# Query features of sketch attention formed by token from 8-vectors: a fused attention and GELU kernel on one core

## The chip, the cores and the metric

The kernel runs on one core of one Trainium2 chip. The metric is the time of one execution on the device in microseconds (us). The engines are named as the profile names them: PE is TensorE (matrix products), PEld its loading of weights, DVE is VectorE, ACT is ScalarE, POOL is GpSimd, and SP is SyncE, whose queue issues the DMAs.

## The reference

Polynomial sketch attention feeds a GELU block. The sizes are 4 batches, 4 heads, 1088 tokens, head width 32, and sketches of 8 rows; the GELU block takes 4352 tokens of width 128 through 2048 hidden units.

```python
def phi(x):
    a = np.einsum('rd,bhsd->bhsr', S1, x)
    b = np.einsum('rd,bhsd->bhsr', S2, x)
    return np.einsum('bhsi,bhsj->bhsij', a, b).reshape(*x.shape[:-1], r * r)
q_p, k_p = (phi(q), phi(k))
kv = np.einsum('bhsf,bhsd->bhfd', k_p, v)
z = np.sum(k_p, axis=2)
num = np.einsum('bhsf,bhfd->bhsd', q_p, kv)
den = np.einsum('bhsf,bhf->bhs', q_p, z)[..., None] + 1e-06
x = (num / den) by token, heads side by side      # 4352 x 128
...
h = x @ w_in
g = 0.5 * h * (1.0 + erf(h * inv_sqrt2))
out = g @ w_out
```

The 64 features of a token are the outer product of two 8-vectors a and b, so the denominator is also the sum over i of a_i times c_i, where c is z (as an 8x8 matrix) applied to b, or in the other order a sketch of the query whose rows are mixed by z. The weights come as double words and are rounded to f32 in the kernel.

## The kernel before, in words

**Chunks.** The queries are taken in nine chunks. Chunks n = 0 to 7 hold 512 tokens of all four heads each, two chunks a batch; chunk 8 is the remainder, the last 64 tokens of each of the four batches (256 columns). For each chunk the attention makes xT, the x of the chunk with its 128 features on partitions, and the GELU block follows.

**Steps.** The whole kernel is one text that fixes the order of instructions on every engine: each instruction is tied to the one before it on its engine (end of the kernel, "order of the text"). The main part is a list of steps t (line 858). One step is one tile of 128 hidden units of one chunk (`hidden`, lines 608 to 627: PE forms h in a bank h_ps, ACT writes its GELU to a block of four tiles). Chunks 0 and 1 share the first 32 steps; then chunk n has steps 16n to 16n+15. A step emits, in this order: drains that are due, the hidden tile, channel differences of a full block (`token_sums`, on POOL), the slot's attention work, stores that are due, then due products. Slots are placed by hand with `at(t, f, ...)`. The attention of chunk n stands among the hidden steps of chunk n-1, at t = 16(n-1) and a little after; below, "hidden step r of a chunk" is step 16n + r.

**Second product.** Four tiles make a block, and a block's share of g @ w_out is formed by a seven-product scheme for 2x2 blocks. `token_sums` (lines 662 to 674) makes four sums of the block's tiles on POOL, `channel_sums` the same of the weights once, and `two_products` (line 690 on, matmuls at L705) adds products in pairs to two banks o_ps, which hold one chunk's sums. The first block's products of a chunk begin at hidden step 6 of the chunk (step 7 of chunk 2). `drain` (lines 709 to 726) reads both banks when a chunk is done, with three ACT copies and six DVE sums, of which the first is L721 and reads the bank that is written first for the next chunk. It is placed at hidden step 5 of the next chunk (step 6 for chunk 1). `store` and `combine` (lines 736 to 780) finish and transpose the chunk on DVE six steps later, and SP issues the output DMAs.

**Keys.** For batches 1 to 3 the key features are made beside odd chunks (n = 3 for batch 2, n = 5 for batch 3; batch 1 earlier): `features_of_all` (PE and ACT), `outer_of_all` (DVE), `kv_sum` (PE), and `turn_kv`, which turns kv and z with the identity and leaves them in kz[b], where z is repeated over 32 columns. Batch 0 is made first in another form (`kv_first`), and `rearrange_kz` copies it on POOL to kz_late for chunk 8.

**Queries, the part that is changed.** `query_turn` (DVE, L495) transposes a chunk's q in blocks of 32x32. `expand_products` (L509) forms both factors of all 64 features with 16 matmuls: the sketches S1 and S2 are repeated to 64 columns in Srep, and each matmul uses 32 rows and 64 columns of the array with 256 columns of data. `expand_copy` (ACT, L516) copies the first factor out of the banks, and `expand_multiply` (DVE, L522; L528 for chunk 8) multiplies by the second. `attend` (lines 539 to 560) has four matmuls of 64 rows, 64 columns and 512 columns of data (L549) that give the numerators and, through the repeated z, the denominators in 32 equal rows; ACT copies the denominators with 1e-6 added (L555), DVE takes their reciprocal (L556) and multiplies it into the numerators, one head at a time (L560). Chunks 0 and 1 are made by token instead (`numerators_by_token`, `divide`) in the kernel's first part, which the change leaves alone. In the banks' pool `w_ps` two buffers of two banks serve all of this attention work in turn.

Of the kernel before, what the change touches and what calls it, by code (L numbers as in the profile page):

```python
# [16 lines left out]
def kernel(  # L17
# [29 lines left out]
    JC = 4  # L47
# [42 lines left out]
    rem = {n: big.tile([128, B // 2, H, D], FP, name=f"{n}_rem") for n in "qkv"}  # L90
# [19 lines left out]
    def load_q(n):  # L110
        at = n % NCH * CW
        if n < NCH:
            sp.dma_start(out=q_sb[n], in_=q[0, :, at:at + CW, :].rearrange("h (p j) d -> p h j d", j=JC))
            return
        src = q[n // NCH, :, at:at + CW, :].rearrange("h (t g j) d -> g t h (j d)", g=G, j=JC)
        for g in range(G):
            sp.dma_start(out=q_sb[n][g * 32:(g + 1) * 32].rearrange("t h j d -> t h (j d)"), in_=src[g])
# [72 lines left out]
    def load_rest():  # L190

        load_w_out(1, gated=True)
        for i in range(2, len(pieces)):
            load_w_in(i)
            load_w_out(i)
        for b in range(1, B):
            load_turned_k(b)
            load_main(sp, "v", b)
            for c in range(NCH):
                load_q(b * NCH + c)  # L200
            if b == 1:
                for n, b1 in (("k", 1), ("k", 3), ("v", 1), ("v", 2), ("v", 3)):
                    load_rem(n, b1)
        for b in range(B):
            load_rem("q", b)
# [13 lines left out]
    def kz_cols(b, h):  # L219

        c, r = h // 2, h % 2
        return (r * 2 * D, r * 2 * D + D) if b == 0 else ((2 * r + c) * D, (2 * r + 1 - c) * D)


    kz_late = big.tile([128, 128], FP, name="kz_late")

    def rearrange_kz():
        to, of = (x.rearrange("f (r two d) -> f r two d", r=2, two=2) for x in (kz_late, kz[0]))
        for c in range(NP):
            rows = slice(c * F, (c + 1) * F)  # L230
            pool.tensor_copy(out=to[rows, :, c], in_=of[rows, :, 0])
            pool.tensor_copy(out=to[rows, :, 1 - c], in_=of[rows, :, 1, 0:1].broadcast_to([F, 2, D]))
# [217 lines left out]
    def kv_product(ps, lhsT, features, b, h, part, start=False, stop=False):  # L450

        at, c = kz_cols(b, h)[part], h // 2
        pe.matmul(ps[at:at + D, c * F:(c + 1) * F], lhsT=lhsT, rhs=features, start=start, stop=stop, skip_group_check=True)  # L453

    def kv_sum(b, ps):


        for i in range(J):
            ch, t, one = i % 2, i // 4, i // 2 % 2
            for h in range(H):  # L460
                kv_product(ps, main["v", b][:, h, i, :], flat(k_p[b, h % 2][:, t, h // 2 * 4 + ch * 2 + one]), b, h, 0,
                           start=i == 0)
        for h in range(H):
            kv_product(ps, v_rem_aug[b][:, h, :], flat(k_p_rem[b % 2][:, h]), b, h, 0, stop=True)
        if b == 1:
            for h in range(H):
                kv_product(ps, ones_rem, flat(k_p_rem[b][:, h]), b, h, 1)
        for m in range(2 if b == 1 else 1):
            for h in range(H):
                kv_product(ps, ones, k_s[h % 2][:, h // 2, 0, m], b, h, 1, stop=b > 1 or m == 1)  # L470
# [7 lines left out]
    def turn_kv(b, ps):  # L478
        for rows in (slice(0, 64), slice(64, 128)):
            pe.matmul(ps[rows, :128], lhsT=kv_T[b][:, rows], rhs=ident, start=True, stop=True)  # L480
        act.copy(out=kz[b], in_=ps[:, :128])

# [4 lines left out]
    def query_turn(n, copy=by_act):  # L487


        if n == 1:  # L490
            turned = transposed(work_bank(), "qT", [q_sb[1][:, h].rearrange("p j d -> p (j d)") for h in range(H)], copy)
            qT[n] = turned.rearrange("p (h j t) -> p h j t", h=H, j=JC)
            return
        qT[n] = att.tile([128, H, width[n] // 128, D], FP, name="qT" if n < NMAIN else "qT_rem")
        dve.transpose(out=qT[n], in_=q_sb[n] if n < NMAIN else rem["q"].rearrange("p i h d -> p h i d"))  # L495
# [22 lines left out]
    def expand_multiply(n, i):  # L518
        W = width[n]
        a, b = (t.rearrange("f g (r x) -> f g r x", r=2) for t in (A[i][:, :, :W // 2], B_of[n, i][:, :, W // 2:W]))  # L520
        if n < NMAIN:
            dve.tensor_mul(out=qp[n].rearrange("f r (g x) -> f g r x", g=G)[:, 2 * i:2 * i + 2], in0=a, in1=b)  # L522
            return

        cols = qp[n][:, :, :W].rearrange("f r (j g t) -> f g r j t", g=G, t=32)
        a, b = (x.rearrange("f g r (j t) -> f g r j t", t=32) for x in (a, b))
        for g in range(2):
            dve.tensor_mul(out=cols[:, 2 * i + g], in0=a[:, g], in1=b[:, g])  # L528
# [5 lines left out]
    def query_expand(n):  # L534
        expand_products(n)
        for i in range(2):
            query_features(n, i)

    def attend(n, meanwhile=lambda: None):


        W = width[n]
        owners = [(0, W, n // NCH)] if n < NMAIN else [(i * REM, (i + 1) * REM, i % 2 * 2 + i // 2) for i in range(B)]
        banks = halves(work_banks())
        for (c0, c1, b) in owners:
            for r in range(2):
                for c in range(NP):
                    to, m = r * 2 * D, 2 * D
                    pe.matmul(banks[c][to:to + m, c0:c1], lhsT=(kz[b] if b else kz_late)[c * F:(c + 1) * F, to:to + m],  # L549
                              rhs=qp[n][c * F:(c + 1) * F, r, c0:c1], start=True, stop=True)  # L550
        meanwhile()
        den = att.tile([128, CW], FP, name="den")
        for h in range(H):
            at = kz_cols(1, h)[1]
            act.activation(out=den[h * D:(h + 1) * D, :W], in_=banks[h // 2][at:at + D, :W], func=ACT.Copy, bias=1e-6)  # L555
        dve.reciprocal(out=den[:, :W], in_=den[:, :W])  # L556
        xT[n] = att.tile([128, CW], FP, name="xT", bufs=3)
        for h in range(H):
            rows, at = slice(h * D, (h + 1) * D), kz_cols(1, h)[0]
            dve.tensor_mul(out=xT[n][rows, :W], in0=banks[h // 2][at:at + D, :W], in1=den[rows, :W])  # L560
# [3 lines left out]
    def numerators_by_token(n, banks, tokens):  # L564

        for at, i in enumerate(tokens):
            for r in range(2):
                for half in range(2):
                    for c in range(NP):
                        rows, col, tok = slice(c * F, (c + 1) * F), (at * 2 + r) * C, i * 128 + half * 64  # L570
                        v_at = kz_cols(0, 2 * c + r)[0]
# [355 lines left out]
    at(18, expand_products, 2)  # L927
    at(18, query_features, 2, 0)
    at(19, query_features, 2, 1)
# [3 lines left out]
    at(24, attend, 2)  # L933
    for i, t in enumerate((25, 26, 28)):
        at(t, channel_sums, i)
    at(6, rearrange_kz)
    for n in range(3, NCHUNK):
# [6 lines left out]
        at(t + 2 if n > 3 else t - 2, query_expand, n)  # L944
# [4 lines left out]
        at(t + 5 + (n == NCH + 1), attend, n, lambda b=b, keys=keys: keys and features_of_all(b))  # L949
        if keys:  # L950
            at(t + 5 + (n == NCH + 1), outer_of_all, b)
# [121 lines left out]
```

## Time and profile before

| what | value |
|---|---|
| median of 3 runs | 270.43 us |
| lowest and highest | 269.98 and 270.69 us |
| span of the profiled execution | 268.4 us, 6204 instructions |
| median of the runs less that span | 2.0 us |
| granted TensorE clock in the span | 0.999 of full |
| busy share: PE, PEld, DVE, ACT, POOL | 98, 51, 55, 51, 65% |
| HBM traffic | 13.1 MB in and out, 49 GB/s over the span |

The profiled execution's own time is given as its span, from the first instruction to the last; the runs' time lies about it. Shares of busy time are over the whole span. A group line gives the source line, engine, operation, output and inputs by name, shapes and count, then busy time and the mean of one in ns, then the idle time of the engine just before these instructions with what ended it. A timeline line gives the start in us from the span's start, the length in us, the instruction, and in brackets the idle time before it. Matmuls overlap, so the mean of one record is longer than the distance from one start to the next; a matmul in f32 leaves two records.

### The profile page before, as it was taken

The numbers are of one execution on the slowest core, as the hardware profiler recorded it, in microseconds if no ns is written. First come the engines' busy times: TensorE is split into PE (matmuls) and PEld (weight loads), VectorE is DVE, ScalarE is ACT, GpSimd is POOL, SyncE is SP. The second block draws the span as 40 slices with busy tenths as digits, with TensorE's granted clock in tenths as the row PEclk, the third lists the DMA queues.
The fourth block names the chain that finished last, engine by engine and source line by source line (L and its number), as shares of the span: only waits on it lengthen the run. The fifth ranks groups of instructions, "written<-read, shape, count | busy, mean of one in ns | idle before, by whom it ended". The sixth has DMA issues, their size and how long they took to land.

```text
span 268.4 us, 6204 instructions
## 1 busy us (share of the span) xinstructions
PE 263.2 (98%) x2529; PEld 137.6 (51%) x2529; DVE 148.5 (55%) x248; ACT 136.5 (51%) x272; POOL 174.2 (65%) x184
## 2 busy tenths in 40 slices
PE   8999999999999999999999999999999999999994
PEld 6844444344454545444445445454444444445794
DVE  3985888506784698189114993387018801750240
ACT  4664766545635533573348333663357334633441
POOL 3512008899997589767864899667866786777300
PEclk9999999999999999999999999999999999999999
DMA  6489263626101000200200002000100020010020
GB/s 203 130 246 326 62 167 70 165 68 171 34 2 29 12 0 5 36 4 0 42 1 2 0 2 42 0 2 10 29 2 1 2 39 0 2 26 16 1 42 20
DMA packets 37869, 13.52 MB, mean 50 GB/s; under 512 B 28240, under 2 KB 37200, under 8 KB 37840
## 3 DMA queue, kind: packets, MB, share of 16 engines
q1 hardware_dynamic: 37648, 13.05, 19.3%
q8 instruction: 20, 0.33, 0.5%
q10 hardware_dynamic: 192, 0.07, 0.1%
q14 instruction: 9, 0.07, 0.1%
HBM read 10.88 MB, written 2.23 MB: 49 GB/s over the span
## 4 chain that ended last, share of the span: by engine, by line
PE 95%; DVE 2%; ACT 0%; issue 0%; DVEq 0%
PE h_ps L620 44%; PE o_ps L705 32%; PE o_ps L756 5%; PE w_ps L509 3%; PE w_ps L753 3%; PE w_ps L549 3%; PE w_ps L453 2%; PE w_ps L787 1%; PE w_ps L374 1%; PE h_ps L332 1%; DVE bits_a L272 1%; DVE q_pT L522 0%; PE w_ps L572 0%; DVE x_tok L593 0%; PE h_ps L635 0%
## 5 line engine op out<-in xcount | busy, mean ns | idle before, releaser
L620 PE MATMUL h_ps<-xT,w_in 128*64 128x512 f32 (+3 forms) x516 | 139.9, 577 | 0.0
L627 ACT ACTIVATE block<-h_ps 128x512 f32<-128x512 f32 (+1 forms) x128 | 72.8, 571 | 101.6 <-PE h_ps L620 98.5
L705 PE MATMUL o_ps<-block,w_out 128*64 128x256 f32 x224 | 57.9, 381 | 0.0
L620 PEld LDWEIGHTS h_ps<-xT,w_in 128*64 128x64 f32 (+1 forms) x516 | 41.8, 143 | 28.6 <-issue 8.1
L670 POOL TENSOR_TENSOR bits_low<-block 128x512 f32<-128x512 f32 x28 | 36.2, 1295 | 22.7 <-ACT block L627 22.4
L705 PEld LDWEIGHTS o_ps<-block,w_out 128*64 128x64 f32 x224 | 30.0, 137 | 36.9 <-issue 27.6
L671 POOL TENSOR_TENSOR bits_a<-block 128x512 f32<-128x512 f32 x28 | 36.5, 1304 | 15.2 <-ACT block L627 15.1
L673 POOL TENSOR_TENSOR bits_m<-block,bits_e 128x512 f32<-128x512 f32 x28 | 36.2, 1293 | 2.2
L672 POOL TENSOR_TENSOR bits_e<-bits_a,block 128x512 f32<-128x512 f32 x28 | 36.0, 1287 | 2.2
L556 DVE RECIPROCAL den<-den 128x512 f32<-128x512 f32 (+1 forms) x7 | 21.9, 3122 | 14.0 <-ACT den L555 14.0
L522 DVE TENSOR_TENSOR q_pT<-A_sb,w_ps 128x512 f32<-128x512 f32 x16 | 10.3, 683 | 34.0 <-ACT A_sb L516 34.0
L705 PE MATMUL o_ps<-bits_a,small 128*64 128x256 f32 x112 | 29.0, 382 | 0.0
L705 PE MATMUL o_ps<-bits_m,w_out 128*64 128x256 f32 x112 | 28.8, 380 | 0.0
L705 PE MATMUL o_ps<-bits_low,small 128*64 128x256 f32 x112 | 28.7, 379 | 0.0
L705 PE MATMUL o_ps<-block,small 128*64 128x256 f32 x112 | 28.7, 379 | 0.0
L721 DVE TENSOR_TENSOR sums<-o_ps,sums 64x512 f32<-64x512 f32 x8 | 5.5, 682 | 35.9 <-ACT sums L718 20.4
L705 PEld LDWEIGHTS o_ps<-block,small 128*64 128x64 f32 x112 | 15.3, 137 | 18.0 <-issue 12.8
L560 DVE TENSOR_TENSOR xT<-w_ps,den 32x512 f32<-32x512 f32 (+1 forms) x28 | 18.2, 648 | 1.0
L705 PE MATMUL o_ps<-bits_e,small 128*64 128x256 f32 x112 | 16.8, 379 | 0.0
L756 PE MATMUL o_ps<-g,w_out 128*128 128x512 f32 x32 | 16.4, 599 | 0.1
L555 ACT ACTIVATE den<-w_ps 32x512 f32<-32x512 f32 (+1 forms) x28 | 15.6, 558 | 1.3 <-PE w_ps L549 1.0
L705 PEld LDWEIGHTS o_ps<-bits_low,small 128*64 128x64 f32 x112 | 15.3, 137 | 0.0
(167 smaller groups left out, 313.9 us busy)
## 6 DMA issues: line engine op xcount, KB each, us to landing
block<-in_moe_w_in_dram SPq DMA_DIRECT2D x3, 512.0 KB, 7.7
block<-in_moe_w_out_dram SPq DMA_DIRECT2D x3, 512.0 KB, 10.6
k<-in_k_dram SPq DMA_DIRECT2D x48, 32.0 KB, 1.9
v<-in_v_dram SPq DMA_DIRECT2D x3, 512.0 KB, 4.0
q<-in_q_dram SPq DMA_DIRECT2D x24, 64.0 KB, 3.4
out_dram<-oT SPq DMA_DIRECT2D x24, 64.0 KB, 2.2
k<-in_k_dram SPq DMA_DIRECT2D x2, 256.0 KB, 3.0
q<-in_q_dram SPq DMA_DIRECT2D x2, 256.0 KB, 3.9
```

Of the source, the lines that this page charges most:

```text
L522: dve.tensor_mul(out=qp[n].rearrange("f r (g x) -> f g r x", g=G)[:, 2 * i:2 * i + 2], in0=a, in1=b)
L555: act.activation(out=den[h * D:(h + 1) * D, :W], in_=banks[h // 2][at:at + D, :W], func=ACT.Copy, bias=1e-6)
L556: dve.reciprocal(out=den[:, :W], in_=den[:, :W])
L560: dve.tensor_mul(out=xT[n][rows, :W], in0=banks[h // 2][at:at + D, :W], in1=den[rows, :W])
L620: pe.matmul(ps[rows, :W], lhsT=w[:, rows], rhs=xT[n][:, :W], start=True, stop=True)
L627: act.activation(out=g_of[n, fi][:, :W], in_=ps[:, :W], func=ACT.Gelu)
L670: pool.tensor_sub(out=s[3], in0=a11, in1=a21)
L671: pool.tensor_add(out=s[1], in0=a21, in1=a22)
L672: pool.tensor_sub(out=s[2], in0=s[1], in1=a11)
L673: pool.tensor_sub(out=s[4], in0=a12, in1=s[2])
L705: pe.matmul(acc[n][bank][half * 64:(half + 1) * 64, col:col + HW], lhsT=fixed, rhs=moving, start=opens and e == 0 and name in "4715", stop ...
L756: pe.matmul(o_of[n], lhsT=w_tile(w_out_sb, fi), rhs=g, start=first, stop=final)
```

## The change

For chunks 2 to 8 the query features are formed by token.

- **z goes into a sketch.** `spread_sketches` builds, on POOL at step 11, a weight tile S_abc for each batch: for a row pair of heads, 32 columns that hold 4 rows of S1, 4 columns for c, and the 8 rows of S2. `sketch_of_z` fills c on DVE (a product of z with S2's columns, a sum over 8, and a product into place) once z of the batch is turned. `turn_kv` now turns only kv, and z is taken from its untransposed form. For batch 0 `turn_first_kv` (step 60, in place of `rearrange_kz`) has ACT copy kv, POOL repeat z's column, and PE turn it.
- **Sketch.** `query_sketch` has eight matmuls of 64 rows, 32 columns and 256 columns of data (chunk 8: sixteen of 64 columns) in place of the sixteen of `expand_products`.
- **Features.** `query_outer` does on DVE what follows: it transposes the banks so that tokens lie on partitions, multiplies a by c, sums to half a denominator, has the other half summed across neighbouring groups of 32 partitions, adds the halves and 1e-6, takes the reciprocal of 32 values a partition, multiplies it into a, forms the outer product of a and b (128x1024) and transposes it back.
- **Numerators.** `attend` has eight matmuls of 64 rows, 32 columns and 256 columns of data that give x^T itself, and ACT copies it to xT.
- **Loads.** q is loaded so that a partition holds 16 consecutive tokens of one head; the remainder of q comes in 16 DMAs in place of 4.
- **Places.** Sketch and features stand at t+2 for odd n and t+4 for even n (before: expansion at t+2, for n = 3 at t-2); `attend` at t+9 and t+11 (before: t+5, for n = 3 at t+6). For chunk 2 they stand at steps 23 and 29 (before 18, 19 and 24).

```diff
@@ load_q
-        src = q[n // NCH, :, at:at + CW, :].rearrange("h (t g j) d -> g t h (j d)", g=G, j=JC)
-        for g in range(G):
-            sp.dma_start(out=q_sb[n][g * 32:(g + 1) * 32].rearrange("t h j d -> t h (j d)"), in_=src[g])
+        for h in range(H):
+            sp.dma_start(out=q_sb[n][h * 32:(h + 1) * 32].rearrange("t x j d -> t (x j d)"),
+                         in_=q[n // NCH, h, at:at + CW, :].rearrange("(t n) d -> t (n d)", t=32))
...
@@ turn_kv
-            pe.matmul(ps[rows, :128], lhsT=kv_T[b][:, rows], rhs=ident, start=True, stop=True)
+            pe.matmul(ps[rows, :128], lhsT=kv_T[b][:, :F], rhs=ident, start=True, stop=True)
         act.copy(out=kz[b], in_=ps[:, :128])
+        sketch_of_z(b, kv_T[b][:, F:])
...
+    def turn_first_kv():
+        of = kz[0].rearrange("f (r x) -> f r x", r=2)
+        to = kz_first.rearrange("f (c r d) -> f c r d", c=NP, r=2)
+        for c in range(NP):
+            act.copy(out=to[:F, c], in_=of[c * F:(c + 1) * F, :, 0:D])
+        zs = att.tile([128, 2, D], FP, name="z_cols")
+        pool.tensor_copy(out=zs, in_=of[:, :, D:C].broadcast_to([128, 2, D]))
+        ps = work_bank()
+        for h in range(H):
+            c, r = h // 2, h % 2
+            pe.matmul(ps[h * D:(h + 1) * D, :F], lhsT=zs[:, r], rhs=ident[:, c * F:(c + 1) * F], start=True, stop=True)
+        sketch_of_z(0, ps[:, :F])
...
+    def query_sketch(n):
...
+        for s in range(2):
+            for i in range(m):
+                for fh in range(2):
+                    for c in range(NP):
+                        rows, q4 = slice(c * 64, (c + 1) * 64), 2 * s + fh
+                        pe.matmul(ps[q4 * 32:(q4 + 1) * 32, c, i * N:(i + 1) * N],
+                                  lhsT=S_abc[batch_of(n, s, i)][rows, fh].rearrange("p r x -> p (r x)"),
+                                  rhs=qT[n].rearrange("p h j t -> p (h j t)")[rows, (s * m + i) * N:(s * m + i + 1) * N],
+                                  start=True, stop=True)
+        sketched[n] = ps
+
+    def query_outer(n):
...
+        dve.transpose(out=tok[:, :W].rearrange("p (c x) -> p c x", c=NP), in_=sketched.pop(n)[:, :, :W // 2])
+        x = tok[:, :W].rearrange("p (k x) -> p k x", x=2 * R)
+        a, c, b = x[:, :, 0:4], x[:, :, 4:8], x[:, :, 8:16]
...
+        dve.tensor_mul(out=m, in0=a, in1=c)
...
+        dve.tensor_reduce(out=part, in_=m, axis=mybir.AxisListType.X, op=AX.add)
+        for g in range(4):
+            dve.tensor_reduce(out=other[(g ^ 1) * 32:((g ^ 1) + 1) * 32], in_=m[g * 32:(g + 1) * 32], axis=mybir.AxisListType.X,
+                              op=AX.add)
+        dve.tensor_add(out=part, in0=part, in1=other)
+        dve.tensor_scalar(out=part, in0=part, scalar1=1e-6, scalar2=None, op0=AX.add)
+        dve.reciprocal(out=part, in_=part)
+        dve.tensor_mul(out=m, in0=a, in1=part[:, :, None].broadcast_to([128, K, 4]))
...
+        dve.tensor_mul(out=feat.rearrange("p (k i j) -> p k i j", i=4, j=R), in0=m[:, :, :, None].broadcast_to([128, K, 4, R]),
+                       in1=b[:, :, None, :].broadcast_to([128, K, 4, R]))
...
+        dve.transpose(out=qp[n].rearrange("f r x -> f (r x)")[:, :2 * W], in_=feat)
...
@@ attend
+        for i in range(m):
+            for s in range(2):
+                rows, b = slice(s * 64, (s + 1) * 64), batch_of(n, s, i)
+                for h in range(H):
+                    pe.matmul(banks[h * D:(h + 1) * D, s, i * N:(i + 1) * N],
+                              lhsT=(kz[b] if b else kz_first)[rows, h * D:(h + 1) * D],
+                              rhs=f[rows, h // 2, i, :, h % 2], start=True, stop=True)
         xT[n] = att.tile([128, CW], FP, name="xT", bufs=3)
+        act.copy(out=xT[n][:, :W].rearrange("p (s x) -> p s x", s=2), in_=banks[:, :, :W // 2])
...
@@ places
+    at(23, query_sketch, 2)
+    at(23, query_outer, 2)
+    at(29, attend, 2)
...
+    at(11, spread_sketches)
+    at(60, turn_first_kv)
...
-        at(t + 2 if n > 3 else t - 2, query_expand, n)
+        at(t + 2 + (n % 2 == 0) * 2, query_sketch, n)
+        at(t + 2 + (n % 2 == 0) * 2, query_outer, n)
...
-        at(t + 5 + (n == NCH + 1), attend, n, lambda b=b, keys=keys: keys and features_of_all(b))
+        at(t + 9 + (n % 2 == 0) * 2, attend, n)
```

## Prediction

> **What bounds the kernel now.** I read the page's shares first, then the chain of work that ended last, then TensorE's groups by form, then the order of time round one place. Page, engines and chain:
>
> ```profile
> PE 263.2 (98%) x2529; PEld 137.6 (51%) x2529; DVE 148.5 (55%) x248; ACT 136.5 (51%) x272; POOL 174.2 (65%) x184
> ...
> PE 95%; DVE 2%; ACT 0%; issue 0%; DVEq 0%
> ...
> L556 DVE RECIPROCAL den<-den 128x512 f32<-128x512 f32 (+1 forms) x7 | 21.9, 3122 | 14.0 <-ACT den L555 14.0
> ```
>
> TensorE (PE) never rests, and the chain is PE for 95%. So a saving on VectorE (DVE) or ScalarE (ACT) is worth nothing by itself; a PE saving counts in full, and so does every new wait of PE. The span is 268.4 us; the runs' median, 270.43, lies 2.0 above it. All terms below are differences, so I add them to the median.
>
> PE's groups by form (busy us, mean ns):
>
> ```profile
> L509 PE MATMUL w_ps<-qT,Srep 32*64 32x256 f32 x256 | 9.0, 387 | 0.0
> L453 PE MATMUL w_ps<-k_p,v 128*32 128x64 f32 x192 | 3.3, 220 | 0.0
> L549 PE MATMUL w_ps<-q_pT,kz 64*64 64x512 f32 x48 | 6.5, 614 | 0.0
> ```
>
> **What PE saves.** Each matmul leaves two records. Per chunk L509 has 32 records of 256 columns on 8 tiles, 1024 columns a tile, and L549 8 of 512 on 4 tiles, also 1024. Start to start, from the timeline, they cost 1.15 us (108.12 to 109.27) and 1.12 us (114.05 to 115.17). The new sketch and numerators each have 16 records of 256 columns on eight 64x32 tiles: 512 columns a tile. Half of 1.05 plus 0.1 for the change of tile is 0.62 each, so a chunk saves 2.27 - 1.24 = 1.03 us. Ends: L453 shows 32-wide tiles running four at a time (17 ns a record of 64 columns); were four the limit here too, the saving would be nothing; with no switching cost it is 1.23. I take 1.03, since L509 does run eight at a time. Six chunks (2 to 7) give 6.2; the remainder, 1.5 before, takes 64 records at 17 ns = 1.1, so 0.4 more; turn_first_kv adds 8 records, 0.3. **Net -6.3 us** (0 to -7.5).
>
> **What else leaves or comes at nothing.** Per chunk ACT loses 4 den copies and 2 A copies and gains one xT copy, and DVE loses reciprocal, 4 quotients and 2 products. PE's 98% hides these already. The q loads keep number and bytes; the q remainder issues 16 DMAs where 4 took 2.58 us, some 8 us more on SP after 67.0, and the next entry there is a store at 79.92: hidden, at most a late store of the first chunk. spread_sketches (six small POOL operations, 0.1 to 0.3 each by POOL's smallest rows) stands at step 11, twelve steps ahead of its reader.
>
> **What PE will wait for.** DVE works in the order of the text. The chunk's new DVE chain, query_outer, stands at t+2 (odd n) or t+4 (even n); the drain of the chunk before last stands at t+5, behind it. The next chunk's first product L705 reuses the drained bank, so it waits for the drain's first DVE operation, L721. Before, for n=4 (DVE, then PE; hidden steps at 113.19 and 115.17):
>
> ```profile
> 114.26 0.68 DVE L721 TENSOR_TENSOR sums<-o_ps,sums 64x512 f32<-64x512 f32 x1 [2.98 <-PE h_ps L620]
> ```
> ```profile
> 113.19 1.03 PE L620 MATMUL h_ps<-xT,w_in 128*64 128x512 f32 x4
> 114.15 1.09 PE L549 MATMUL w_ps<-q_pT,kz 64*64 64x512 f32 x8
> 115.17 1.08 PE L620 MATMUL h_ps<-xT,w_in 128*64 128x512 f32 x4
> 116.08 0.38 PE L705 MATMUL o_ps<-block,small 128*64 128x256 f32 x1
> ```
>
> The drain's first operation ends at 114.94 and PE comes for the bank at 116.08: 1.1 us in hand, and DVE had stood idle 2.98 us. Afterwards the chain fills that idle time. Behind the waiting product stand all of PE's hidden steps, so the wait moves the end.
>
> Length of query_outer, 128 partitions, from DVE rows: turn 128x512, as L768, 0.70; product 128x128, as L593, 0.28; reduce, no row, 0.28 as any 128-element operation (0.86 at the reciprocal's 6.5 ns an element, hardly less than 0.2); four reduces on 32 partitions 1.0; sum, scalar 0.18 each, as L587; reciprocal of 32 elements 0.35 (203 ns for 8, 253 for 16); product 0.28; features 128x1024 1.22, from 683 and 417 ns for 512 and 256; turn 1.22 from 704 and 446; nine dependent starts at 0.05. Sum **6.1 us**. Four of its operations read two SBUF operands. Such operations show this while POOL runs:
>
> ```profile
> 75.63 0.41 DVE L739 TENSOR_TENSOR sums<-sums 64x256 f32<-64x256 f32 x1
> 76.05 1.41 DVE L740 TENSOR_TENSOR sums<-sums 64x256 f32<-64x256 f32 x1
> 77.50 1.65 DVE L742 TENSOR_TENSOR sums<-sums,g 128x512 f32<-128x512 f32 x1
> ```
>
> The same 64x256 sum takes 0.41 or 1.41, and 512 columns 1.65 against 0.69 for L296. L739, L740, L419 and L422 together lie about 0.45 above their shortest: 0 to 1.06 each. Four give +1.8 (0 to 4.2): 7.9 in all; the remainder, at half width, 4.3 + 1.8 = 6.1. The Trainium skill, "SBUF — State Buffer", section "Who interferes with whom", speaks against this change: a VectorE instruction with two SBUF inputs and a GpSimd one reading SBUF exclude each other for a whole instruction. It agrees with the 1.41 here; by it alone each could wait a full 1.3 us POOL operation, +5.2 a chunk instead of 1.8.
>
> The stall is the chain + 0.8 (L721 and a hand-over), less PE's own work from sketch to opening, in hidden steps of 0.86 (start to start), product pairs of 0.43, key products of 1.0:
> - n=4 and 6: two pairs, two hidden steps, 2.7. 7.9 + 0.8 - 2.7 = 6.0 each.
> - n=8: 6.1 + 0.8 - 2.7 = 4.2.
> - n=5: 6.6 of work, 2.1. n=7, no keys: 5.6, 3.1.
> - n=3: 8.3 of work, but store(0)'s combine, 4.2 (75.63 to 79.9), stands between too: 7.9 + 4.2 + 0.8 - 8.3 = 4.6.
> - The other bank follows when the drain ends, 2.3 after; PE has 2.15 of work: 0.15 six times, 1.0.
>
> Sum 27.0. The numerators themselves wait for nothing: seven steps, some 11 us, lie between sketch and attend.
>
> **A second wait, on POOL.** turn_first_kv (step 60, chunk 3's hidden step 12) has PE wait for a POOL copy queued behind the channel differences of hidden step 11. In before that step starts at 124.26 and POOL works on:
>
> ```profile
> 126.01 1.40 POOL L671 TENSOR_TENSOR bits_a<-block 128x512 f32<-128x512 f32 x1 [0.45 <-ACT block L627]
> 127.49 1.27 POOL L672 TENSOR_TENSOR bits_e<-bits_a,block 128x512 f32<-128x512 f32 x1
> 128.84 1.27 POOL L673 TENSOR_TENSOR bits_m<-block,bits_e 128x512 f32<-128x512 f32 x1
> ```
>
> The copy (as L231, 0.34) ends at 130.5; PE is there after 0.86 + 0.62 + 0.43 + 0.86, at 127.0. **3.5 us**, once; nothing if POOL were free.
>
> **The clock after a stall.** No row shows a long rest of PE inside the kernel. Nearest is its start:
>
> ```profile
> 0.77 2.90 PE L787 MATMUL w_ps<-const-float32-0.0 128*128 128x256 f32 x6 [0.77 <-PEq L1057]
> 3.73 1.09 PE L332 MATMUL h_ps<-ident,k 128*128 128x128 f32 x4
> ```
>
> Six records of 256 columns took 2.9 where 0.215 each is usual, then four of 128 took 0.9 to the next start against 0.43: about 1.7 us lost. So 0 to 1.7 a stall. A stall is shorter than a launch; I take half, 0.85, for the four above 4 us: **+3.4**. The Trainium skill, "TensorE: Matmul & The Clock Gate", section "What's actually happening", has an idle window of about 3.4 us halve the clock until one has been busy. Every stall of 3.5 or more would then cost 1.7: five of them, 8.5 in place of 3.4.
>
> **Sum.** -6.3 + 27.0 + 3.5 + 3.4 = +27.6: 270.4 + 27.6 = **298 us**.
>
> **Rivals.**
> - DVE free of POOL (6.1 and 4.3): stalls 2.8, 4.2, 4.2, 2.4, 0.3, 1.3, second bank 1.0, POOL 3.5 give 19.7, less 6.3, no clock loss: 283.8. For: L739 at 0.41. Against: POOL's channel differences run exactly then.
> - The clock falls at every stall: 298 - 3.4 + 7 x 1.7 = 306.5. For: the start rows. Against: the stalls at n=5 and 7 are short.
> - Reduces at 6.5 ns an element: five at 0.86 instead of 1.28 together, +3.0 on six chains: about 315. Against: other one-pass operations take 1 ns.
> - Not slower: the drain isn't held up, and PE keeps its 6.3: 264.1. This needs query_outer under 1.9 us in even chunks and under 3.3 to 5.8 in odd ones (the work above less 0.8, and less 4.2 for n=3); its first and last turns alone make 1.92. It is decided at those six openings.
> - The smaller tiles don't run eight at a time: no saving, some 304; inside the range.
>
> **Chances.** Forecast (290 to 303) 0.50, DVE free 0.20, clock 0.17, slow reduces 0.09, not slower 0.04. A measurement of this kernel tells about 0.3% from no change. Faster 0.03, same 0.01, slower 0.96. The range runs from the free DVE's 283 to 313, past the clock's case, and leaves out the longest chains and the not slower case.
>
> **What would show it.** In the changed profile: PE busy with the two query groups near 1.2 a chunk; PE idle before L772 (the products' new line) released by DVE L788 (the drain) at six places, longest for n=4 and 6; one idle stretch before L516 released by POOL; the 128x1024 product above 1.2 us; slower matmuls straight after the long stalls. I am wrong if DVE ends the drains before PE's openings, or if the chain of waits stays 95% PE.

## The result, and the profile after

The changed kernel takes 309.09 us (median of 4 runs, 308.14 to 311.65) where the kernel before took 270.21 in the same session (269.96 to 270.69). The ratio is 1.1436, 95% interval 1.137 to 1.1503. The profiled execution took 308.48 us; its span is 306.7, 38.3 longer than the 268.4 of before. The forecast of 298 was 11 too low, inside its range.

The page of the changed kernel: engines, the clock granted to PE in 40 slices of 7.67 us, and the chain that ended last.

```profile
PE 272.1 (89%) x2489; PEld 138.0 (45%) x2489; DVE 153.9 (50%) x300; ACT 118.3 (39%) x239; POOL 176.8 (58%) x188
...
PEclk9999999999988999699999999779995999789999
...
PE 76%; DVE 19%; issue 2%; POOL 1%; ACT 1%; DVEq 0%; POOLq 0%; ACTq 0%
```

Two things are new. PE's share fell from 98 to 89%, and the chain now runs for 19% through DVE: PE waits. And PE's *busy* time rose by 8.9 us, although it has 40 records fewer. The second line tells why: in places the clock is at 0.5 to 0.8. Before, the whole span had 0.999.

Who is waited for (us in total, times, longest):

```profile
PE o_ps L772 <- DVE sums L788: 26.5, 6, 5.3
PE w_ps L516 <- POOL z_cols L512: 2.9, 1, 2.9
```

These are the six waits at the chunks' opening products and the one wait at the turn of z, 29.4 us in all. The products of chunk 3 open beside the attention of chunk 4; this opening (below, n=4) on DVE's timeline (start, length, instruction, in brackets the idle time ahead):

```profile
118.16 0.72 DVE L591 STREAM_TRANSPOSE A_sb<-w_ps 128x512 f32<-128x512 f32 x1 [4.57 <-PE w_ps L580]
118.91 0.80 DVE L595 TENSOR_TENSOR q_ac<-A_sb 128x128 f32<-128x128 f32 x1
...
122.06 0.88 DVE L604 TENSOR_TENSOR q_ac<-A_sb,q_den 128x128 f32<-128x128 f32 x1
122.97 1.23 DVE L606 TENSOR_TENSOR q_f<-q_ac,A_sb 128x1024 f32<-128x1024 f32 x1
124.23 1.25 DVE L609 STREAM_TRANSPOSE q_pT<-q_f 128x1024 f32<-128x1024 f32 x1
125.40 0.64 DVE L788 TENSOR_TENSOR sums<-o_ps,sums 64x512 f32<-64x512 f32 x1
```

and on PE's:

```profile
118.90 1.89 PE L687 MATMUL h_ps<-xT,w_in 128*64 128x512 f32 x8
126.10 0.69 PE L772 MATMUL o_ps<-block,small 128*64 128x256 f32 x1 [5.31 <-DVE sums L788]
...
127.86 1.06 PE L772 MATMUL o_ps<-bits_e,small 128*64 128x256 f32 x4
128.71 1.92 PE L687 MATMUL h_ps<-xT,w_in 128*64 128x512 f32 x4
...
131.73 1.03 PE L687 MATMUL h_ps<-xT,w_in 128*64 128x512 f32 x4
```

DVE's chain for chunk 4 runs from 118.16 without a gap, the drain's first operation L788 stands behind it, and PE, done at 120.8, waits 5.31 us for it. Then a second loss follows: the same hidden step (four records of 512 columns) takes 1.92 at 128.71 and 1.03 at 131.73. From the opening to the next hidden step but one it is 5.63 us (126.10 to 131.73); in the kernel before it was 3.02 (116.08 to 119.10). So 2.6 us went to a slow clock after the wait, on top of the wait. The table by stretch shows it too (stretch; length, busy time of PE, PEld, DVE, ACT, POOL; granted clock; DMA):

```profile
90.00:100.00 10.00, 9.03 (x68) 4.53 (x70) 9.45 (x18) 3.96 (x12) 5.77 (x6) 0.83 0.20 29
120.00:130.00 10.00, 4.69 (x20) 1.93 (x18) 9.49 (x21) 1.17 (x2) 2.21 (x2) 0.72 0.01 2
...
160.00:170.00 10.00, 7.31 (x62) 2.92 (x58) 9.73 (x14) 2.70 (x8) 5.05 (x5) 1.00 0.01 2
```

After the waits of 2.90 (turn of z, at 142.85) and 2.69 (chunk 5, at 163.47) the clock stayed at 1.00. After the five others, 3.88 to 5.32 long, it fell.

How long it stays low is not set by the wait alone. Read in narrow stretches, the clock changes at 90.35, 93.77, 124.49, 131.31, 196.17, 202.99, 230.30, 237.13, 264.43 and 271.26, and all of these places lie multiples of 3.413 us apart. So the clock is set once for each stretch of a fixed grid. Around the wait of 5.31 (ended at 126.10), then around the wait of 2.90 (139.95 to 142.85):

```profile
121.08:124.48 3.40, 0.00 (x0) 0.00 (x0) 3.19 (x7) 0.35 (x1) 1.28 (x1) 1.00 0.00 0
124.50:127.90 3.40, 1.80 (x10) 1.03 (x12) 3.21 (x6) 0.00 (x0) 0.00 (x0) 0.50 0.00 0
127.91:131.30 3.39, 3.39 (x16) 1.38 (x14) 2.48 (x6) 0.60 (x1) 0.00 (x0) 0.50 0.02 5
131.32:134.72 3.40, 3.40 (x26) 1.66 (x24) 0.00 (x0) 0.79 (x2) 3.21 (x3) 1.00 0.52 77
...
138.14:141.55 3.41, 1.81 (x24) 0.49 (x8) 0.00 (x0) 1.98 (x5) 2.81 (x4) 1.00 0.00 0
141.55:144.97 3.42, 2.12 (x22) 1.17 (x24) 1.66 (x7) 0.00 (x0) 1.25 (x2) 1.00 0.00 0
```

After a stretch of the grid in which PE did nothing the clock is 0.50. It is 0.50 again after a stretch with 1.80 of work, and back at 1.00 after a busy one. The wait of 2.90 lay across two stretches with 1.6 and 1.3 of it in each, and nothing fell.

Compared in the same way, opening to next hidden steps, the losses are 1.4 (n=3), 2.6 (4), 0.2 (5), 2.5 (6), 2.6 (7), 2.7 (8): **12.0 us**. All but the 0.2 of n=5, which came at full clock, are the clock's, 11.8. The account of the 38.3 us is then: idle waits 29.4, plus 0.17 at each of the seven from the wait's end to the product's pace, 1.2; losses after the waits 12.0; query work saved on PE, -4.8 (below). Sum 37.8; a wait of 0.3 for z's sketch, ahead of chunk 2's query sketch, makes it 38.1.

### The profile page after: what moved, and what is told of

The parts are those of the page before. It is cut to its first block, busy times and chain, and to the rows that moved or that the text cites. A ratio compares the mean times of both kernels' runs of the same rounds, so it can differ in the third digit from the quotient of the medians.

```text
span 306.7 us, 6132 instructions
## 1 busy us (share of the span) xinstructions
PE 272.1 (89%) x2489; PEld 138.0 (45%) x2489; DVE 153.9 (50%) x300; ACT 118.3 (39%) x239; POOL 176.8 (58%) x188
## 4 chain that ended last, share of the span: by engine, by line
PE 76%; DVE 19%; issue 2%; POOL 1%; ACT 1%; DVEq 0%; POOLq 0%; ACTq 0%
PE h_ps L687 33%; PE o_ps L772 28%; PE o_ps L823 5%; DVE q_f L606 3%; PE w_ps L820 2%; DVE q_den L599 2%; DVE q_ac L604 2%; DVE q_ac L595 2%; PE w_ps L580 1%; DVE q_pT L609 1%; PE w_ps L446 1%; DVE A_sb L591 1%; PE w_ps L623 1%; DVE sums L788 1%; DVE q_den L601 1%
## 5 line engine op out<-in xcount | busy, mean ns | idle before, releaser
L687 PE MATMUL h_ps<-xT,w_in 128*64 128x512 f32 (+3 forms) x516 | 142.3, 591 | 0.0
L772 PE MATMUL o_ps<-block,w_out 128*64 128x256 f32 x224 | 59.7, 390 | 0.0
L772 PE MATMUL o_ps<-block,small 128*64 128x256 f32 x112 | 33.7, 429 | 26.5 <-DVE sums L788 26.5
L591 DVE STREAM_TRANSPOSE A_sb<-w_ps 128x512 f32<-128x512 f32 (+1 forms) x7 | 4.8, 679 | 65.4 <-PE w_ps L580 65.4
L772 PE MATMUL o_ps<-bits_low,small 128*64 128x256 f32 x112 | 33.7, 430 | 0.0
L772 PE MATMUL o_ps<-bits_a,small 128*64 128x256 f32 x112 | 30.6, 398 | 0.0
L772 PE MATMUL o_ps<-bits_e,small 128*64 128x256 f32 x112 | 19.4, 428 | 0.0
L788 DVE TENSOR_TENSOR sums<-o_ps,sums 64x512 f32<-64x512 f32 x8 | 5.3, 659 | 25.5 <-ACT sums L785 25.5
L772 PEld LDWEIGHTS o_ps<-bits_a,small 128*64 128x64 f32 x112 | 16.3, 148 | 0.0
L772 PEld LDWEIGHTS o_ps<-bits_m,w_out 128*64 128x64 f32 x112 | 14.7, 137 | 0.0
L772 PEld LDWEIGHTS o_ps<-bits_e,small 128*64 128x64 f32 x112 | 8.6, 153 | 12.9 <-issue 10.5
```

Source lines behind the costliest of these rows:

```text
L591: dve.transpose(out=tok[:, :W].rearrange("p (c x) -> p c x", c=NP), in_=sketched.pop(n)[:, :, :W // 2])
L687: pe.matmul(ps[rows, :W], lhsT=w[:, rows], rhs=xT[n][:, :W], start=True, stop=True)
L772: pe.matmul(acc[n][bank][half * 64:(half + 1) * 64, col:col + HW], lhsT=fixed, rhs=moving, start=opens and e == 0 and name in "4715", stop ...
L788: dve.tensor_add(out=C[lo, 1], in0=a1[lo], in1=C[lo, 0])
```

## The experiments

The theory at this point: all of the loss is waits of PE behind DVE's query_outer (and one behind POOL), set by the places in the text, plus a clock that falls when PE rests for some 3 us. Rivals: the new matmul tiles themselves lower the clock or PE's pace; the waits only move when one is taken away; DVE's work would be too long wherever it stands.

**1. Other places for the same work.** Sketch and features are moved so that DVE's chain doesn't stand just ahead of a drain.

```diff
-        at(t + 2 + (n % 2 == 0) * 2, query_sketch, n)
-        at(t + 2 + (n % 2 == 0) * 2, query_outer, n)
+        early = t - 1 if n == 3 else t - 4 if n % 2 else t + 6
+        at(early, query_sketch, n)
+        at(early, query_outer, n)
...
-        at(t + 9 + (n % 2 == 0) * 2, attend, n)
+        at(t + 9 + (n % 2 == 0) * 4, attend, n)
```

> The changed kernel with sketch and features moved so that no drain stands behind them on VectorE: even chunks at hidden step 6 (after the drain), odd chunks from 5 on at hidden step 12 of the chunk before, chunk 3 at step 31; numerators of even chunks two steps later. Theory (PE waits behind the drain and then loses clock): 26.5 of the 29.4 us of PE idle and some 12 us of half clock go, the 2.9 us wait on POOL stays: 270 to 273 us, granted clock 0.99 or more. Rival (the 64x32 tiles themselves lower the clock or run slowly): the waits go, the clock stays near 0.95: about 283 us. Rival (the VectorE chain is too long wherever it stands): new waits elsewhere, over 290 us.

Measured 277.12 us, ratio 1.0253 (1.0226 to 1.028). The waits of PE in it:

```profile
PE w_ps L516 <- POOL z_cols L512: 3.8, 1, 3.8
PE o_ps L772 <- DVE sums L788: 3.5, 1, 3.5
```

Five of the six openings no longer wait, with the same work on every engine: 32 us come back from an edit of a few lines. It stayed some 4 us above what was expected, because two waits are left, one of them at a place that the move didn't free (the opening of chunk 2's products, beside chunk 3's chain). Both are followed by a slow clock (0.66 in 88 to 98, 0.83 in 134 to 144). The account: -4.8 saved, waits 7.3, 0.17 at each of two, and the two falls as this trace has them, 2.7 (half clock from the wait's end at 89.58 to 95.00) and 1.7 (from 135.96 to 139.37), make 7.2, and the 0.3 for z's sketch 7.5. The span grew by 8.0 (276.4 against 268.4), so 0.5 stays open.

**2. The copy of z ten steps earlier.** On POOL's timeline of the changed kernel the 0.24 us copy stands behind a block's four differences:

```profile
136.92 1.28 POOL L737 TENSOR_TENSOR bits_low<-block 128x512 f32<-128x512 f32 x1 [1.54 <-ACT block L694]
...
141.36 1.26 POOL L740 TENSOR_TENSOR bits_m<-block,bits_e 128x512 f32<-128x512 f32 x1
142.56 0.24 POOL L512 COPY z_cols<-kz 128x64 f32<-128x64 f32 x1
```

```diff
-        zs = att.tile([128, 2, D], FP, name="z_cols")
-        pool.tensor_copy(out=zs, in_=of[:, :, D:C].broadcast_to([128, 2, D]))
+        zs = z_cols[0]
...
+    at(50, spread_first_z)
```

(`spread_first_z` holds the two lines that are taken out.) It was tried by itself and with the order of experiment 1.

> The changed kernel with only POOL's copy of z's column moved from step 60 to step 50, ahead of the channel differences. Theory: PE's 2.9 us idle at the turn of batch 0's z goes and nothing else changes: 3 us less than the changed kernel, 305 to 306.5 us. Rival (the wait only moves to the next drain): under 1 us.

> Both moves. Theory: no PE wait above 1 us is left, clock 0.99 or more, and what stays is the smaller PE work: the two query groups cost 0.74 us each start to start in the changed kernel, 1.48 against 2.27 a chunk, so 264.5 to 267 us, faster than the kernel before. Rival (smaller tiles lower the clock): about 280 us.

By itself: 308.38 us, ratio 1.1389 (1.1332 to 1.1447), 0.7 less than the changed kernel between medians whose runs overlap. The wait on the copy is gone from its list, but the openings take more:

```profile
PE o_ps L778 <- DVE sums L794: 28.0, 6, 5.3
```

They take 1.5 us more. Of these 1.24 are chunk 7's (5.12 against 3.88), where the chain's addition of 1e-6 takes 1.30 beside POOL in place of 0.18, and 0.28 are chunk 5's, the next opening. A wait of 0.73 for POOL also appears at 58.6, ahead of the edit's place. The slow clock after the waits costs 13.6 in place of 11.7, since the waits lie otherwise on the grid and the one of 2.97 at chunk 5 now makes it fall. So the time fits the rival, under 1 us, but its mechanism accounts for 0.3 us. Whether the rest comes from the edit or from chance, one trace doesn't show.

With the new order: 272.59 us, ratio 1.0067 (1.0032 to 1.0101), 4.5 less than the order alone. In the traces the wait of 3.8 is gone, and with it the 1.7 of slow clock behind it. The same edit was worth 0.7 and 4.5 us in the two settings. It missed its expectation by some 6 us for the wait at chunk 2's products that experiment 1 had left:

```profile
PE o_ps L778 <- DVE sums L794: 3.5, 1, 3.5
```

With the clock that falls after it (0.86 in 90 to 100; half speed from 89.47 to 92.78 costs 1.7) and the 0.17 at its end that wait accounts for 5.4. The ten runs show the grid without a trace: the clock over the span was 0.999 in two (270.27 and 270.49 us), 0.993 or 0.994 in six (272.10 to 273.90) and 0.987 in two (273.17 and 273.52). One slow stretch of 3.41 is 0.006 of such a span, so the same program had none, one or two of them.

**3. The waits filled.** To part the clock from the waits, the changed kernel got matmuls of noughts into an unused bank ahead of the products' openings of chunks 2 to 7 and of the turn of z, as many as fit the wait. They change nothing that is read.

```diff
+                keep_busy({2: 11, 3: 11, 4: 5, 5: 11, 6: 8, 7: 9}[n], work_bank())
...
+        keep_busy(6, ps)
```

> The changed kernel with matmuls of zeros put on PE just ahead of each opening product and of the turn of z (11, 11, 5, 11, 8, 9 and 6 matmuls of 128x128 by 256 columns, 0.43 us each), sized to the idle time there; the waits themselves stay. Theory (the clock falls because PE rests): clock 0.99 or more in every stretch, and the 12 us of half clock go: 296 to 299 us. Rival (the smaller tiles lower the clock): clock 0.95, 308 us or more.

Measured 299.3 us (298.37 to 301.23), ratio 1.1076 (1.1028 to 1.1124): **9.8 us less by work that is thrown away**. The stretches that had 0.83 and 0.72:

```profile
90.00:100.00 10.00, 9.42 (x77) 4.78 (x77) 9.23 (x18) 4.29 (x12) 5.78 (x6) 1.00 0.20 29
120.00:130.00 10.00, 9.67 (x56) 6.18 (x54) 9.54 (x19) 1.47 (x3) 3.00 (x3) 1.00 0.00 0
```

DVE is as busy as it was, so the openings are about as late; only the clock is back at 1.00. That is the clock's part of the loss by a second way. It is 2.0 under the 11.8 read from the trace. Some 1.2 of that is a longer wait at n=7: from the last hidden step to the opening it is 5.71 where it was 4.47, and the chain's addition of 1e-6 again takes 1.30 beside POOL in place of 0.18. The rest stays open.

**4. Rests in the kernel before.** This has none of the new tiles. Reciprocals on a scratch tile are put on DVE ahead of five drains, ever more of them, so that PE rests there.

```diff
+            at(t + 2, spend, {4: 5.0, 5: 7.0, 6: 7.2, 7: 8.1, 8: 9.4}[n])
```

> The kernel before, tiles and all, with idle reciprocals on VectorE ahead of the drains that come in the attention of chunks 4 to 8 (5.0, 7.0, 7.2, 8.1 and 9.4 us), so that PE should wait about 1, 2, 3, 4 and 5 us at these openings. Theory (order on VectorE alone makes the wait, and rests of PE above some 3 us cost about 2.5 us of half clock more): 15 us of waits and 5 to 8 of clock: 290 to 294 us, granted clock 0.97 to 0.98. Rival (the clock falls through the smaller tiles only): clock 0.999 and 285 to 286 us.

Measured 291.72 us, ratio 1.0768 (1.0725 to 1.0812). PE's timeline shows the rests, 0.69, 1.88, 2.98, 3.85 and 4.87; the first three:

```profile
116.90 0.43 PE L705 MATMUL o_ps<-block,small 128*64 128x256 f32 x1 [0.69 <-DVE sums L721]
...
148.25 0.43 PE L705 MATMUL o_ps<-block,small 128*64 128x256 f32 x1 [1.88 <-DVE sums L721]
...
181.44 0.43 PE L705 MATMUL o_ps<-block,small 128*64 128x256 f32 x1 [2.98 <-DVE sums L721]
183.49 1.92 PE L620 MATMUL h_ps<-xT,w_in 128*64 128x512 f32 x4
```

and the clock after them:

```profile
150.00:155.00 5.00, 5.00 (x38) 2.44 (x36) 4.87 (x5) 1.79 (x3) 3.85 (x4) 1.00 0.00 0
...
180.00:185.00 5.00, 3.56 (x16) 1.68 (x18) 4.77 (x9) 0.52 (x1) 1.26 (x1) 0.71 0.00 0
215.00:220.00 5.00, 4.61 (x24) 2.28 (x26) 4.80 (x7) 0.60 (x1) 0.11 (x1) 0.66 0.00 0
```

Full speed after 1.88, about half after 2.98, 3.85 and 4.87 (0.63 in 250 to 255). The rests add up to 14.3, the span grew by 21.0; less 0.17 at each of five, 5.9 remain for three falls of the clock. In the trace they are one slow stretch of 3.41 each after 2.98 and 3.85 (182.06 to 185.47, 216.19 to 219.61), 1.7 lost, and 2.1 after 4.87 (from 249.54 to 253.74), 5.5 in all. The rival that the clock falls through the new tiles only is out.

**5. DVE without POOL beside it.** The changed kernel without `token_sums`' four differences; the products read a tile of noughts in their place, so that part of the second product is left out of the output. PE's work is the same.

```diff
-        pool.tensor_sub(out=s[3], in0=a11, in1=a21)
-        pool.tensor_add(out=s[1], in0=a21, in1=a22)
-        pool.tensor_sub(out=s[2], in0=s[1], in1=a11)
-        pool.tensor_sub(out=s[4], in0=a12, in1=s[2])
-        sums[n, b] = s
+        sums[n, b] = fixed
```

> The changed kernel without POOL's channel differences of the GELU blocks: the products that use them take a tile of noughts instead, so these parts of the result are left out; the number and form of PE's products stay. If VectorE's two-input operations wait for POOL, L595, L601, L604 and L606 fall to 0.28, 0.19, 0.28 and 1.23 us, the scalar sum L602 to 0.18, and the chain from its first turn to the drain to 6.2 us in every full chunk (7.2 to 8.8 in those of the changed kernel looked at); the wait at the turn of z goes; waits at the even openings stay at 4.2 to 4.5 us: 287 to 293 us. If POOL has no part in it, the chain stays above 7 us and only z's wait goes: 303 to 306 us.

Measured 284.73 us (one run), 24 less than the changed kernel; the openings wait 13.2 us in five, and the wait for z is gone. This lies 2.3 under the range that theory gave. The chain was foreseen: 6.14 us in chunks 4, 6 and 7 where 6.2 was expected, with waits of 4.22 at the even openings. DVE's groups by form, mean ns after the busy time; first the changed kernel, then this one:

```profile
L606 DVE TENSOR_TENSOR q_f<-q_ac,A_sb 128x1024 f32<-128x1024 f32 x6 | 10.5, 1746 | 0.2
L599 DVE TENSOR_REDUCE q_den<-q_ac 32x32 f32<-32x128 f32 x24 | 6.7, 277 | 0.3
L595 DVE TENSOR_TENSOR q_ac<-A_sb 128x128 f32<-128x128 f32 x6 | 5.0, 839 | 0.2
...
L602 DVE TENSOR_SCALAR q_den<-q_den 128x32 f32<-128x32 f32 x6 | 3.2, 538 | 0.2
```

```profile
L606 DVE TENSOR_TENSOR q_f<-q_ac,A_sb 128x1024 f32<-128x1024 f32 x6 | 7.4, 1225 | 0.2
L599 DVE TENSOR_REDUCE q_den<-q_ac 32x32 f32<-32x128 f32 x24 | 6.7, 277 | 0.3
L595 DVE TENSOR_TENSOR q_ac<-A_sb 128x128 f32<-128x128 f32 x6 | 1.8, 292 | 0.2
...
L602 DVE TENSOR_SCALAR q_den<-q_den 128x32 f32<-128x32 f32 x6 | 1.1, 181 | 0.2
```

Beside POOL the 128x128 product takes nearly three times as long, and the one-input addition of 1e-6 too; the reduces don't change by a nanosecond. With the sum L601 (676 against 193) and the product L604 (932 against 292) the operations that wait lose 2.55 us a chunk on average.

**6. The last wait.** Order and z as in 2, and chunk 2's first products two steps later.

```diff
-            late = int(n < NCH or n == NCH and opens)
+            late = 3 if n == NCH and opens else int(n < NCH)
```

> Both moves of order_and_z, and the first block's products of chunk 2 begin at its hidden step 9 instead of 7, so that PE comes 3.4 us later for the bank that chunk 3's VectorE chain holds up. Theory: the last wait, 3.5 us, and the 1.4 to 2 us of half clock after it go; the smaller PE work stays: 266.5 to 268.5 us, 0.7 to 1.5% faster than the kernel before, clock 0.997 or more. Rival (the saving on PE isn't real): 270 us or more with no wait left.

Measured 272.38 us, ratio 1.0071 (1.0046 to 1.0095): no gain over 272.59. PE now waits for an ACT block:

```profile
PE h_ps L693 <- ACT block L700: 3.7, 1, 3.7
```

ACT's timeline there:

```profile
81.94 0.60 ACT L700 ACTIVATE block<-h_ps 128x512 f32<-128x512 f32 x1 [0.61 <-PE h_ps L693]
85.65 0.58 ACT L790 COPY sums<-o_ps 64x512 f32<-64x512 f32 x1 [3.11 <-DVE sums L813]
88.06 0.37 ACT L791 COPY sums<-o_ps 64x256 f32<-64x256 f32 x1 [1.83 <-DVE oT L841]
...
88.72 0.59 ACT L700 ACTIVATE block<-h_ps 128x512 f32<-128x512 f32 x1
```

The drain's copies on ACT write tiles named sums, which chunk 0's combine still holds: DVE comes to it (L813 at 84.15, L841 at 87.26) only behind chunk 3's chain. ACT waits in order, and the GELU of the hidden steps stands behind. So the chain delays PE in two ways, and later products open only one of them.

**7. Chunk 0 finished first.** In place of the wait the work ahead of the chain is moved: chunk 0's store comes four steps earlier, chunk 3's sketch and features one step later than in 1, chunk 2's products one step later than in the change.

```diff
+        early = t if n == 3 else t - 4 if n % 2 else t + 6
...
+            late = 2 if n == NCH and opens else int(n < NCH)
...
-                done[t + 12].append(n)
+                done[t + (8 if n == 0 else 12)].append(n)
```

> order_and_z, and in the one place where PE still waited (opening of chunk 2) the first chunk's combine and store stand four steps earlier, straight after its drain, so that the next drain's copies find their tile free; chunk 3's sketch stands behind it at step 32, and chunk 2's first products begin one step later (8). Theory: PE comes for the bank at about 87.5 us and VectorE's drain begins between 84 and 88, so at most 1.6 us of wait is left and no half clock: 266 to 268 us, clock 0.998 or more, 0.8 to 1.6% faster than the kernel before. Rival (the saving on PE isn't real): 270 us with no wait left.

Measured 270.53 us, ratio 0.9986 (0.9962 to 1.001), level with the kernel before and 2.5 above the range. One wait of 2.18 is left, more than expected, as the chain there takes 10.7 us (77.93 to 88.67) while POOL forms blocks' sums without a pause. In the traced run the clock stayed at 1.000. In six of twelve runs it did, with spans of 267.2 to 268.4; in the others the clock over the span was 0.991 to 0.994, and the spans were 269.0 and more. The difference is that of one slow stretch, 1.7. In the traced run the rest of 2.18 lay across two stretches of the grid, 1.5 and 0.7; with all of it in one it would be near the 2.1 after which the clock fell elsewhere. So a rest of this length can go either way; how long it was in the runs without a trace isn't known.

**8. One operation less in the chain.** As 7, with two of the operations that wait for POOL made one:

```diff
-        dve.tensor_add(out=part, in0=part, in1=other)
-        dve.tensor_scalar(out=part, in0=part, scalar1=1e-6, scalar2=None, op0=AX.add)
+        dve.scalar_tensor_tensor(out=part, in0=part, scalar=1e-6, in1=other, op0=AX.add, op1=AX.add)
```

> The same, and the sum of the two half denominators and 1e-6 is one instruction with two SBUF inputs instead of a sum and a scalar sum (0.19 + 0.18 us bare, 0.68 + 0.54 on average beside POOL). The chain gets 0.2 to 1.3 us shorter in each chunk. Theory: if no PE wait is left in store_first, nothing is gained, within 0.3 us; if a wait of up to 1.6 us is left, that much.

Measured **267.43 us** (267.0 to 268.92, 6 runs), ratio 0.9885 (0.9855 to 0.9915): faster than the kernel before, and 41.7 us faster than the change as it was made. PE is back at 98%:

```profile
PE 259.7 (98%) x2489; PEld 134.2 (50%) x2489; DVE 155.6 (59%) x293; ACT 118.2 (44%) x239; POOL 178.9 (67%) x188
```

Two waits of 0.8 are left. The gain over 7 was 3.1 between medians where at most 1.6 was expected; with a rest of 0.84 in place of 2.18 the clock was 0.998 to 1.000 in all six runs, which accounts for the surplus at least in part. The account: -4.8 + 1.7 + 0.3 = -2.8, and the span is 2.4 under that of before.

## Why the prediction was right or wrong, step by step

**Right: the mechanism, its places and the sum of its waits.** Six openings behind the drain and one turn of z were named, with PE's queue behind them. Predicted were 27.0 + 3.5 = 30.5; measured 29.4 idle, 30.6 from start to start. Undoing only the places takes five openings away (experiment 1), undoing only the copy's place takes the seventh (2). By chunk, predicted and measured idle: n=3 4.6 and 5.16; n=4 6.0 and 5.31; n=5 2.1 and 2.69; n=6 6.0 and 5.32; n=7 3.1 and 3.88; n=8 4.2 and 4.16; z 3.5 and 2.90. The 1.0 for the second bank wasn't seen as idle time.

**Nearly right, by errors that cancel: query_outer.** Predicted 7.9 us in a full chunk. In the trace, from the first turn to the start of L788: 7.24 for n=4 and n=6, 8.85 for n=5, 8.82 for n=7; chunk 8's smaller chain 6.04 against 6.1. At n=3 it took 10.23, and chunk 0's combine behind it 2.3 where 4.2 was expected, so that wait came out near by luck. The bare chain was right: for n=4 two of its operations were held by 0.51 and 0.59, and 7.24 less 1.10 is 6.14 against 6.1. The wait for POOL was put at 1.8 for four operations; these lose 2.19 on average, and L602, an addition with one input that wasn't counted, 0.36 more (in single cases it takes 1.21 to 1.30 against 0.18). In even chunks it is less, 1.1: POOL is busy for only 2.21 of the 10 us from 120, since the resting PE makes no block for it. The Trainium skill, "SBUF — State Buffer", section "Who interferes with whom", lists `tensor_scalar` among the operations that can take the shared ports and says that `tensor_reduce` never does; experiment 5 agrees with both (538 and 181; 277 and 277), and the prediction had used only its sentence on two inputs.

**Wrong: the step "The clock after a stall", +3.4.** It measured 11.8 by the trace, 9.8 by experiment 3. Two choices in it failed. The bound of 1.7 a stall, from the launch, is no bound: four of the stalls lost 2.5 to 2.7, for after a rest of 5.3 the records are slow from 126.10 to about 131.3, the rest of two stretches of the grid. The launch rows themselves give more than was read from them: six records of 256 columns and four of 128 took 3.84 (0.77 to 4.61) where 1.72 is usual, 2.1 lost. And half the bound was taken because a stall is shorter than a launch; the length above some 3 us hardly mattered, a wait of 3.88 lost as much as one of 5.32. That term alone is 8.4 of the 10.7 by which the sum of +27.6 fell short of the span's +38.3; the PE saving is 1.5 of it, 0.3 is the wait for z's sketch, which wasn't foreseen, 0.2 came after the wait at n=5, and 0.1 lies in the seven waits. So 309.09 lies outside the 290 to 303 that had the chance of 0.50. The rival "the clock falls at every stall", 306.5, came nearest in time, but not by its condition: the clock didn't fall at the two short waits, and the five falls cost 2.4 each, not 1.7.

The Trainium skill, "TensorE: Matmul & The Clock Gate", section "What's actually happening", which the prediction had set against its own 0.85, was nearer: its idle window of about 3.4 us fits inside five of the measured waits, and at an estimated 1.7 each they make 8.5. The prediction named five by it too, with the turn of z in place of n=7. The page also says that the window runs freely, not from the rest's start, and the grid of 3.41 in the traces agrees. One thing differs: the page has a whole idle window, and here a stretch of the grid with 2.08 us of rest was enough.

**Mis-sized: the PE saving, -6.3.** It measured about -4.8. The two groups show 1.33 of busy time a chunk, where near 1.2 was expected, and cost more from start to start:

```profile
188.44 1.03 PE L687 MATMUL h_ps<-xT,w_in 128*64 128x512 f32 x4
189.40 0.66 PE L580 MATMUL w_ps<-qT,S_abc 64*32 64x256 f32 x16
...
190.90 1.03 PE L687 MATMUL h_ps<-xT,w_in 128*64 128x512 f32 x4
```

From 188.44 to 190.90 are 2.46; less a hidden step and a pair of products at their usual pace (0.86 each) it is 0.74 a group, not 0.62. So 0.79 a chunk where 1.03 was taken: 4.7 for six, with 0.4 and -0.3 taken as predicted. The tiles do run eight at a time; the rival that they don't falls.

**The other rivals.** "DVE free of POOL", 283.8, comes near where POOL is in fact silent, 284.73 in experiment 5, but in part by luck: the openings of n=4 to 8 waited within 0.3 of what it said (4.2, 0, 4.2, 1.2, 2.3), while n=3 waited 1.2 and not 2.8, z's wait of 3.5 wasn't there, and the clock lost 4.3 where the rival had none. Reduces at 6.5 ns an element: no, 286 ns for 128 elements. "Not slower" at 264.1 didn't come: DVE ended no drain before PE came. Taken at nothing, and rightly so: ACT's work, 18.2 us less busy, changed no wait of PE.

**Left open:** the 0.2 us between the account and the span, the 0.5 of experiment 1, and what parts the rest of the 9.8 from the 11.8.

## What to carry to other kernels

Before work is moved between engines, look at what stands behind its new place in each queue: a 7 us chain on an engine that is half idle cost most of 38 us of span because a drain stood behind it, and the same work two to six steps away, with z's copy, one store and one block of products moved too and one operation fewer, made the kernel 1.15% faster than before. Price a wait of the matrix engine at its length plus slow clock where it is about 3 us or longer (1.4 to 3.0 us here, by where it lay on the grid), and take the longest waits first or fill them. When a wait goes, look in the same trace for the next one behind it: one edit was worth 0.7 us with the other waits there and 4.5 without them, and only a part of that is explained.

## What the hardware showed that was not expected

- The granted clock is set for stretches of 3.41 us on a fixed grid, in each trace with a fall inside the kernel. Leaving out the kernels' starts and ends, it fell to 0.50 after every stretch in which PE rested for 2.08 us or more, and after none with 2.02 or less. It came back after stretches with 0.62 of rest or less, and not after 0.74 or more. So a rest of 2.97 lowered it (2.96 of it in one stretch) and one of 2.90 didn't (1.6 and 1.3).
- After rests of 2.98 and 3.85 the first products still ran at full speed (0.43) until the next place on the grid, 0.6 and 0.8 us later. After rests of 3.50 (experiment 1) and 5.31 that place lay inside the rest, and PE began slow (0.69).
- Matmuls of noughts that nobody reads kept the clock up and made the kernel 9.8 us faster.
- A small addition with one SBUF input and constants (128x32) waits for POOL as the two-input ones do: 538 ns on average beside POOL, 181 without.
